# Two elementwise steps of the first units on GpSimd in place of VectorE

## The chip, the cores and the metric
The kernel runs on one core of one Trainium2 chip. The metric is the device time of one execution in microseconds, from a set of repeated runs; lower is better. A profiled execution, from which all rows below come, has its own time beside the span from its first to its last instruction. The engines are named as the profile names them: PE (TensorE), DVE (VectorE), ACT (ScalarE), POOL (GpSimd), SP (the queue that issues the DMAs).

## The reference
Three stages follow each other. A linear attention with a complex decay for each step and channel, over 4 batches, 8 heads, 768 steps and a head size of 48; a dense layer of 384 to 2048 to 384 with a piecewise quadratic activation; and a mixture of 8 experts of 384 to 1024 to 384, mixed by a table that is normalized by rows and columns in turn.

```python
# attention, for each b, h; a = a_re + i a_im
mag = sqrt(a_re**2 + a_im**2)
a_n = a * min(mag, 0.999) / (mag + 1e-6)
for t in range(768):
    S = a_n[t][:, None] * S + outer(k[t], v[t])
    y[t] = q[t] @ S.real
# dense layer on x = y with heads side by side: 3072 x 384
h = x @ w_in
g = where(h >= 1, h, where(h <= -1, 0, (h + 1)**2 / 4))
x2 = g @ w_out
# experts
P = exp(x2 @ w_gate - max); 8 times: rows to sum 1, columns to sum 1, times 3072 / 8
out = sum over e of P[:, e] * (relu(x2 @ w1[e]) @ w2[e])
```

## The kernel before
The time axis is cut into 6 chunks of 128 steps, and a chunk into two units of two batches, so there are 12 units (u = 0 to 11), each of 256 rows of the 384-wide activations. Attention and dense layer go unit by unit; the experts follow when all are done.

A unit's attention has three parts. `attn_norm` (lines 191 to 226) makes the decay's factor, `min(mag, 0.999) / (mag + 1e-6)`, once for each of the unit's two batches, and multiplies the decay tile `A` (real and imaginary part) by it at line 223. `attn_front` (233 to 335) transposes `A` to have time along the free axis (`flip`, 258), forms the products of all decays up to each step by a tree of complex multiplications (`cmul`, 277 to 287, all on VectorE from SBUF to SBUF), transposes back, and scales q and k by them (321 and 331). Its k tile `kh` has 32 columns of padding that GpSimd sets to zero (242); that tile has one buffer, so the padding of a unit is set after the state matmuls of the unit before (393) have read it. `attn_back` (339 to 430) does the attention matmuls of the chunk, masks the scores on VectorE (367, which reads PSUM), and makes the unit's input to the dense layer as two tiles, `x0h` and its rest `x0l`.

The matrix products of both later stages are made with values that are split into a rounded part and the rest of it: `gh` and `gl`, `x0h` and `x0l`, and two planes of each weight tile. Three products of such parts stand for one of full precision.

The dense layer `moe1` (473 to 529) goes over the 16 column blocks of `w_in` in 8 pairs. Each pair has 18 matmuls of line 116 into one PSUM tile; ScalarE makes the activation in three steps (488 to 490), VectorE finishes it (491, which reads PSUM and SBUF) into `t`, ScalarE rounds it into `gh` (494), and VectorE makes the rest `gl` (495). TensorE reads a pair's `gh` and `gl` two pairs later (line 498, `LAG1 = 2`; the matmuls of line 509). `t` has two buffers, `gh` and `gl` three each. During unit 0 the 16 weight tiles are loaded as well (`load_w_moe`, 449 to 471), two for a pair: a tile's raw data come by DMA into one of three staging buffers, which the decay tiles `A` use too; VectorE takes them apart in three instructions (456, 457, 460), ScalarE makes the rounded plane (464), TensorE and ScalarE the second (468 to 470).

The order of the work comes from generators. `weave` (535) draws attention steps of the coming units between the dense layer's steps of the present one, by weights that each generator yields, with `RATIO = 1.2` attention steps' weight for each of the dense layer. `step(u)` (559) runs `attn_back(u)`, `attn_front(u + 1)` and `attn_norm(u + 2)` side by side. From that order the framework's planner makes one queue for each engine, with its own durations and the order of the program as priority. Each engine then runs its queue strictly in order, an instruction waiting on semaphores for what it reads and for buffers to come free.

Before the change GpSimd sets constants, the padding of `kh`, and, from the last unit on, makes sums and differences of the experts' weights and inputs (592 to 595, 652 to 655).

Of the kernel before, what the change touches and what calls it, by code (L numbers as in the profile page):

```python
# [13 lines left out]
ALU = mybir.AluOpType  # L14
# [6 lines left out]
def scan_moe_moe(  # L21
# [14 lines left out]
    nc = tc.nc  # L36
# [20 lines left out]
    M2MIN = 0.97  # L57
    RATIO = 1.2
    NSPLIT = 1
    LAG1 = 2  # L60
    NFIRST = 2
    NWA = 10
# [40 lines left out]
    def f32(ap):  # L103
        return ap.bitcast(F32)
# [4 lines left out]
    def w2p(w, s, c0, n):  # L109
        return w[:, s, DM + c0:DM + c0 + n]  # L110

    def layer1(ps, w, xh, xl):
        n = 0
        for kc in range(KC):
            for s, x in ((0, xh), (0, xl), (1, xh)):
                nc.tensor.matmul(ps, w1p(w, s, kc), x[:, kc, :], start=(n == 0), stop=(n == 3 * KC - 1))  # L116
                n += 1

    def sinkhorn(pool, psp):
# [47 lines left out]
        out=mask, in_=mask, pattern=[[1, 128]], compare_op=ALU.is_ge,  # L167
# [23 lines left out]
    def attn_norm(u):  # L191
        if u < NSPLIT:
            yield from both(norm_part(u, 0, "ns", "nr"), norm_part(u, 1, "qh", "kh"))
        else:
            for b in range(BH):
                yield from norm_part(u, b, "ns", "nr")

    def norm_part(u, b, tag1, tag2):
        A = loaded[u, "a"]
        s12 = ap1.tile([128, 2, DM], F32, name=f"ns{u}_{b}", tag=tag1)  # L200
        r = ap1.tile([128, DM], F32, name=f"nr{u}_{b}", tag=tag2)
        s1, s2 = s12[:, 0], s12[:, 1]
        Ab = A[:, :, b * DM:(b + 1) * DM]
        nc.scalar.activation(s1, Ab[:, 0], AF.Square)
        nc.scalar.activation(s2, Ab[:, 1], AF.Square)
        nc.vector.tensor_tensor_reduce(
            out=s1, in0=s1, in1=s2, op0=ALU.add, op1=ALU.min, scale=1.0, scalar=3.0e38,
            accum_out=mins[:, u * BH + b:u * BH + b + 1],
        )
        yield 0.5  # L210
        nc.scalar.activation(s2, s1, AF.Relu, bias=c_mq)
        nc.scalar.activation(s2, s2, AF.Ln, bias=c_q)
        nc.scalar.activation(r, s2, AF.Exp, scale=-0.5, bias=c_lnh)
        nc.scalar.activation(s2, r, AF.Square, scale=2.0 / MAXMAG)
        nc.vector.tensor_tensor(out=s2, in0=s1, in1=s2, op=ALU.mult)
        yield 0.5
        nc.vector.scalar_tensor_tensor(
            out=r, in0=s2, scalar=3.0, in1=r, op0=ALU.subtract, op1=ALU.mult, reverse0=True
        )
        nc.scalar.activation(s2, r, AF.Identity, scale=-EPS / MAXMAG, bias=c_one)  # L220
        nc.vector.scalar_tensor_tensor(out=r, in0=r, scalar=1.0, in1=s2, op0=ALU.min, op1=ALU.mult)
        yield 1
        nc.vector.tensor_tensor(
            out=Ab, in0=Ab, in1=r.unsqueeze(1).to_broadcast([128, 2, DM]), op=ALU.mult
        )
        yield 1

    def parts(u):
        return [(b, 1) for b in range(BH)] if u < NSPLIT else [(0, BH)]

# [218 lines left out]
    def load_w_moe(f):  # L449
        pool = wpa if f < NWA else wpb  # L450
        if f not in raws:
            raw_w(f)
        st = raws.pop(f)
        w = pool.tile([128, 2, 2 * DM], F32R, name=f"w_m{f}", tag="w")
        lo, hi = st[:, :, 0], st[:, :, 1]
        nc.vector.tensor_scalar(out=lo, in0=lo, scalar1=29, scalar2=None, op0=ALU.logical_shift_right)
        nc.vector.scalar_tensor_tensor(
            out=lo, in0=hi, scalar=3, in1=lo, op0=ALU.logical_shift_left, op1=ALU.bitwise_or
        )
        nc.vector.scalar_tensor_tensor(  # L460
            out=lo, in0=hi, scalar=-(1 << 31), in1=lo, op0=ALU.bitwise_and, op1=ALU.bitwise_xor
        )
        xf = f32(lo)
        nc.scalar.activation(w[:, 0, :], xf, AF.Copy, scale=-(2.0 ** -126))
        for i in range(2):
            sl = slice(i * DM, (i + 1) * DM)
            ps = ps_h.tile([128, DM], F32, name=f"lo{f}_{i}", tag="h")
            nc.tensor.matmul(ps, up, xf[:, sl], start=True, stop=False)
            nc.tensor.matmul(ps, dn, w[:, 0, sl], start=False, stop=True)
            nc.scalar.activation(w[:, 1, sl], ps, AF.Copy, scale=2.0 ** -63)  # L470
        wm[f] = w

    def moe1(u):
        c, bp = divmod(u, B // BH)
        xh, xl = x0.pop(u)
        hh = {}
        NP = NF1 // 2
        for p in range(NP + LAG1):
            if p < NP:
                ps = ps_h.tile([128, 2, UT], F32, name=f"h{u}_{p}", tag="h")  # L480
                for i in range(2):
                    for f in range(min(2 * p + i + 3, NF1)):
                        if f not in wm:
                            load_w_moe(f)
                    layer1(ps[:, i, :], wm[2 * p + i], xh, xl)
                    yield 1
                t = hp.tile([128, 2, UT], F32, name=f"t{u}_{p}", tag="t", bufs=2)
                nc.scalar.activation(t, ps, AF.Relu, bias=c_one, scale=-0.25)
                nc.scalar.activation(t, t, AF.Relu, bias=c_two, scale=-1.0)
                nc.scalar.activation(t, t, AF.Square, scale=0.5)  # L490
                nc.vector.scalar_tensor_tensor(out=t, in0=ps, scalar=0.25, in1=t, op0=ALU.mult, op1=ALU.max)
                gh = hp.tile([128, 2, UT], F32R, name=f"gh{u}_{p}", tag="hh")
                gl = hp.tile([128, 2, UT], F32R, name=f"gl{u}_{p}", tag="hl")
                nc.scalar.activation(gh, t, AF.Copy)  # L494
                nc.vector.tensor_tensor(out=gl, in0=t, in1=f32(gh), op=ALU.subtract)
                hh[p] = (gh, gl)
                yield 0
            if p >= LAG1:
                gh, gl = hh.pop(p - LAG1)
                for i in range(2):  # L500
                    j = 2 * (p - LAG1) + i
                    w = wm[j]
                    for m in range(KC):
                        if j == 0 and m == 0:
                            a01 = ps_a.tile([128, 2, UT], F32, name=f"x2pa{u}", tag="m")
                            a2 = ps_a.tile([128, UT], F32, name=f"x2pb{u}", tag="m")
                            acc = (a01[:, 0], a01[:, 1], a2)
                        for n, (s, g) in enumerate(((0, gh), (0, gl), (1, gh))):
                            nc.tensor.matmul(  # L509
                                acc[m], w2p(w, s, m * 128, 128), g[:, i, :],  # L510
                                start=(j == 0 and n == 0 and m != 1), stop=(j == NF1 - 1 and n == 2 and m != 0),
                                skip_group_check=(m < 2),
                            )
                    yield 1
        lg = psp.tile([128, BH, NE], F32, name=f"lg{u}", tag="m")
        for m in range(KC):
            with tc.high_priority(60):
                xb = x0p.tile([128, UT], F32, name=f"x2b{u}_{m}", tag="x2b", bufs=2)
                nc.scalar.activation(xb, acc[m], AF.Copy, scale=0.25)
                nc.sync.dma_start(x2s[c][:, m, bp * UT:(bp + 1) * UT], xb)  # L520
            for b in range(BH):
                for o in (0, 64):
                    nc.tensor.matmul(
                        lg[o:o + 64, b, :], xb[:, b * T + o:b * T + o + 64], wg[:, m, :],
                        start=(m == 0 and b == 0), stop=(m == KC - 1 and b == BH - 1), skip_group_check=True,
                    )
        j = c * B + bp * BH
        nc.vector.tensor_copy(P[:, j:j + BH, :], lg)
        yield 1
# [20 lines left out]
    def both(*gs):  # L550
        gs = list(gs)
        while gs:
            for g in list(gs):
                try:
                    yield next(g)
                except StopIteration:
                    gs.remove(g)
# [64 lines left out]
    for u in range(NU):  # L622
        while u not in done:
            next(side)
        if u == NU - 1:
            attn.close()
            xrp = main.enter_context(tc.tile_pool(name="xrp", bufs=1, side="right", reuse_waits="tile"))
            load_x2(0)
            load_x2(1)
        weave(moe1(u), side, RATIO)  # L630
# [414 lines left out]
```

## Time and profile before

| | us |
|---|---|
| median of 3 runs | 2310.19 |
| lowest, highest | 2309.71, 2314.92 |
| profiled execution, its own time | 2307.67 |
| its span | 2305.9 |
| PE busy in the span | 2239.6 (97%) |
| PEld (weight loads) | 2145.3 (93%) |
| DVE busy | 1644.2 (71%) |
| ACT busy | 914.0 (40%) |
| POOL busy | 117.3 (5%) |

The shares are means over very different stretches. Up to about 62 us the first unit's attention runs alone; then the dense layer of unit 0 with its weight loads and the attention of unit 1; then eleven units of dense layer with attention beside it; and from about 700 us on the experts. So the rows below are taken by stretch. The profile's granted clock of PE has a mean of 0.993 over the span, and is 0.9 or more of full speed in all of the page's 40 slices but the first.

### The profile page before, as it was taken

What the parts mean: (1) busy time and instruction counts of PE and PEld (TensorE: products, weight loads), DVE (VectorE), ACT (ScalarE), POOL (GpSimd) and SP (SyncE); (2) the same over time, 40 slices, a digit from 0 to 9 for tenths busy, and PEclk for the clock granted to TensorE, in tenths of its full rate; (3) what the DMA queues carried; (4) which work ended last, traced back from release to release, by engine and by line L of the source; (5) the groups of instructions that cost most, each with busy time, mean ns of one, the idle gap of its engine ahead of it and who ended that gap; (6) DMA issues with size and microseconds to landing.
All of it is one profiled execution on the core that took longest, in us unless ns stands there. A gap on an engine that the chain in (4) does not pass through costs nothing.

```text
span 2305.9 us, 40891 instructions
## 1 busy us (share of the span) xinstructions
PE 2239.6 (97%) x16829; PEld 2145.3 (93%) x16829; DVE 1644.2 (71%) x3064; ACT 914.0 (40%) x1641; POOL 117.3 (5%) x178
## 2 busy tenths in 40 slices
PE   3789999999999999999999999999999999999998
PEld 2679999999998999999999999999999999999998
DVE  8898888887754887767866877675575576556554
ACT  5787877776566223222322322232232232222221
POOL 0000000000012010100100200010020010000000
PEclk8999999999999999999999999999999999999999
DMA  7443222211123143431423332231132222221220
GB/s 137 144 97 60 49 45 43 43 29 29 29 83 117 57 150 116 146 110 70 165 96 110 124 110 96 83 137 50 74 138 83 82 71 110 83 83 62 90 110 30
DMA packets 179795, 204.06 MB, mean 88 GB/s; under 512 B 128144, under 2 KB 168592, under 8 KB 173456
## 3 DMA queue, kind: packets, MB, share of 16 engines
q1 hardware_dynamic: 179600, 201.36, 27.2%
q8 instruction: 135, 2.21, 0.4%
q14 instruction: 60, 0.49, 0.1%
HBM read 177.75 MB, written 23.59 MB: 87 GB/s over the span
## 4 chain that ended last, share of the span: by engine, by line
PE 87%; DVE 7%; ACT 3%; DMA 1%; issue 1%; SPq 0%; POOL 0%; DVEq 0%; POOLq 0%; ACTq 0%
PE o L739 35%; PE pF L677 12%; PE pE L677 9%; PE h L116 7%; PE pG L677 6%; PE pH L677 6%; PE x2pa L509 4%; PE x2pb L509 2%; DVE M L277 1%; PE sc L365 1%; DVE M L282 1%; DVE Pk L286 1%; PE y L380 1%; PE kTps L355 1%; PE qTps L355 1%
## 5 line engine op out<-in xcount | busy, mean ns | idle before, releaser
L739 PE MATMUL o<-wB,eg 128*128 128x384 f32 x3072 | 784.2, 336 | 0.0
L739 PEld LDWEIGHTS o<-wB,eg 128*128 128x128 f32 x3072 | 547.1, 188 | 0.0
L739 PE MATMUL o<-wB,el 128*128 128x384 f32 x1536 | 515.6, 336 | 0.0
L723 ACT ACTIVATE eg<-et 128x512 fp32r<-128x512 f32 x384 | 243.0, 633 | 682.8 <-DVE et L719 412.0
L724 DVE SCALAR_TENSOR_TENSOR el<-et,eg 128x512 fp32r<-128x512 f32 x384 | 274.1, 714 | 189.0 <-ACT eg L723 186.7
L739 PEld LDWEIGHTS o<-wB,el 128*128 128x128 f32 x1536 | 288.2, 188 | 0.0
L677 PE MATMUL pE<-xop,wA 128*128 128x512 f32 (+1 forms) x1152 | 234.1, 338 | 0.0
L677 PE MATMUL pF<-xop,wA 128*128 128x512 f32 (+1 forms) x1152 | 234.1, 338 | 0.0
L116 PE MATMUL h<-x0h,w_m 128*128 128x256 f32 x1152 | 230.4, 288 | 0.9 <-ACT x0h L427 0.7
L712 DVE TENSOR_TENSOR u<-pH,sv 128x256 f32<-128x256 f32 x192 | 81.2, 423 | 208.5 <-ACT sv L711 208.3
L711 ACT ACTIVATE sv<-pH 128x256 f32<-128x256 f32 x192 | 73.9, 385 | 381.9 <-PE pH L677 381.9
L677 PEld LDWEIGHTS pE<-xop,wA 128*128 128x128 f32 x1152 | 190.0, 189 | 26.3
L677 PEld LDWEIGHTS pF<-xop,wA 128*128 128x128 f32 x1152 | 190.0, 189 | 26.3
L116 PEld LDWEIGHTS h<-x0h,w_m 128*128 128x128 f32 x1152 | 185.8, 191 | 3.7 <-ACT x0h L427 1.3
L509 PE MATMUL x2pa<-gh,w_m 128*128 128x256 f32 x768 | 179.0, 294 | 10.0 <-ACT gh L494 10.0
L677 PE MATMUL pG<-xop,wS 128*128 128x256 f32 x1152 | 169.1, 283 | 0.0
L719 DVE TENSOR_TENSOR et<-pE,sv 128x512 f32<-128x512 f32 x192 | 132.4, 690 | 48.0 <-PE pE L677 47.2
L116 PE MATMUL h<-x0l,w_m 128*128 128x256 f32 x576 | 165.4, 287 | 1.0 <-DVE x0l L428 1.0
L677 PEld LDWEIGHTS pG<-xop,wS 128*128 128x128 f32 x1152 | 152.1, 192 | 0.0
L509 PEld LDWEIGHTS x2pa<-gh,w_m 128*128 128x128 f32 x768 | 133.6, 192 | 13.4 <-ACT gh L494 11.5
L713 DVE TENSOR_TENSOR sv<-pG,u 128x512 f32<-128x512 f32 x192 | 132.6, 691 | 17.6 <-DVE u L712 0.9
L719 DVE TENSOR_TENSOR et<-pF,sv 128x512 f32<-128x512 f32 x192 | 132.2, 688 | 0.3 <-PE pF L677 0.3
(164 smaller groups left out, 3502.6 us busy)
## 6 DMA issues: line engine op xcount, KB each, us to landing
xop<-x2o SPq DMA_DIRECT2D x42, 2304.0 KB, 8.9
st_e<-in_moe_w_dram SPq DMA_DIRECT2D x64, 384.0 KB, 3.9
x2o<-xop SPq DMA_DIRECT2D x6, 2304.0 KB, 9.6
st_m<-in_moe_w_in_dram SPq DMA_DIRECT2D x16, 384.0 KB, 3.4
st_m<-in_moe_w_out_dram SPq DMA_DIRECT2D x16, 384.0 KB, 4.0
raw<-in_moe_w_in_dram SPq DMA_DIRECT2D x16, 384.0 KB, 3.5
raw<-in_moe_w_out_dram SPq DMA_DIRECT2D x16, 384.0 KB, 4.2
q<-in_q_dram SPq DMA_DIRECT2D x12, 384.0 KB, 4.1
```

Source lines behind the costliest of these rows:

```text
L116: nc.tensor.matmul(ps, w1p(w, s, kc), x[:, kc, :], start=(n == 0), stop=(n == 3 * KC - 1))
L277: nc.vector.tensor_tensor(out=m[:, x], in0=dst[:, x:x + 1].to_broadcast(shp), in1=src, op=ALU.mult)
L355: nc.tensor.transpose(ps[:D2, i, :], src[:, 4 * g + i, :], ident)
L509: nc.tensor.matmul(acc[m], w2p(w, s, m * 128, 128), g[:, i, :], start=(j == 0 and n == 0 and m != 1), stop=(j == NF1 - 1 and n == 2 and m ...
L677: nc.tensor.matmul(ps, w[:, a], op[:, b, o:o + n], start=(first and k == 0), stop=(last and k == 2), skip_group_check=True)
L711: nc.scalar.activation(sv[:, 0], H[:, 0], AF.Copy)
L712: nc.vector.tensor_tensor(out=u, in0=H[:, 1], in1=sv[:, 0], op=ALU.add)
L713: nc.vector.tensor_tensor(out=sv[:, 1:3], in0=G, in1=u.unsqueeze(1).to_broadcast([128, 2, HT]), op=ALU.add)
L719: nc.vector.tensor_tensor(out=t, in0=F, in1=sv[:, 2 * r:2 * r + 2], op=ALU.add)
L723: nc.scalar.activation(xh, tf, AF.Relu)
L724: nc.vector.scalar_tensor_tensor(out=xl, in0=tf, scalar=0.0, in1=f32(xh), op0=ALU.max, op1=ALU.subtract)
L739: nc.tensor.matmul(po[i, b], g[:, b * T:(b + 1) * T], wB[:, s, o2:o2 + DM], start=(f == 0 and n == 0), stop=(f == NF2 - 1 and n == 2),)
```

## The change
In the first four units the rest `gl` is made by GpSimd; in units 1 to 3 (`NSPLIT` is 1) the product of `A` with its factor is made by GpSimd too. Operands, tiles, buffers and the text of the generators stay as they are. That moves 4 x 8 = 32 instructions of 128x512 and 3 x 2 = 6 of 128x768.

```diff
+    NPOOL = 4
...
         nc.vector.scalar_tensor_tensor(out=r, in0=r, scalar=1.0, in1=s2, op0=ALU.min, op1=ALU.mult)
         yield 1
-        nc.vector.tensor_tensor(
+        eng = nc.gpsimd if NSPLIT <= u < NPOOL else nc.vector
+        eng.tensor_tensor(
             out=Ab, in0=Ab, in1=r.unsqueeze(1).to_broadcast([128, 2, DM]), op=ALU.mult
         )
...
                 nc.scalar.activation(gh, t, AF.Copy)
-                nc.vector.tensor_tensor(out=gl, in0=t, in1=f32(gh), op=ALU.subtract)
+                eng = nc.gpsimd if u < NPOOL else nc.vector
+                eng.tensor_tensor(out=gl, in0=t, in1=f32(gh), op=ALU.subtract)
                 hh[p] = (gh, gl)
```

## Rows read from the trace of the kernel before

**Rows 1.** Busy time by stretch: start:end, length, then each engine's busy us (instructions), PE clock, DMA.
```profile
0.00:62.00 62.00, 27.12 (x241) 20.86 (x242) 48.49 (x156) 35.95 (x74) 1.71 (x16) 0.83 0.66 128
70.00:128.00 58.00, 48.40 (x287) 39.75 (x288) 56.22 (x104) 40.42 (x72) 0.00 (x0) 0.97 0.48 154
128.00:170.00 42.00, 35.87 (x382) 31.97 (x381) 37.47 (x86) 33.84 (x68) 0.13 (x1) 1.00 0.49 84
170.00:330.00 160.00, 157.63 (x1737) 150.47 (x1736) 139.65 (x289) 125.62 (x238) 0.38 (x3) 1.00 0.23 45
330.00:2305.90 1975.90, 1965.02 (x14154) 1897.70 (x14152) 1358.95 (x2426) 670.61 (x1179) 115.06 (x158) 1.00 0.26 89
```

**Rows 2.** VectorE in order of time, 100 to 116 us: start, duration, what, shapes.
```profile
100.18 0.95 DVE L223 TENSOR_TENSOR A<-A,nr 128x768 f32<-128x768 f32 x1
101.05 0.95 DVE L457 SCALAR_TENSOR_TENSOR st_m<-st_m 128x768 int32<-128x768 int32 x1
...
112.09 0.97 DVE L460 SCALAR_TENSOR_TENSOR st_m<-st_m 128x768 int32<-128x768 int32 x1
...
115.21 0.70 DVE L495 TENSOR_TENSOR gl<-t,gh 128x512 fp32r<-128x512 f32 x1
115.81 0.97 DVE L460 SCALAR_TENSOR_TENSOR st_m<-st_m 128x768 int32<-128x768 int32 x1
```

**Rows 3.** TensorE in order of time at 113 us, in brackets its idle time before.
```profile
113.16 1.25 PE L468 MATMUL lo<-st_m,up 128*128 128x384 f32 x3 [2.12 <-issue]
```

**Rows 4.** VectorE's groups, 70 to 128 us: busy us, mean ns, idle before.
```profile
L456 DVE TENSOR_SCALAR st_m<-st_m 128x768 int32<-128x768 int32 x11 | 6.2, 565 | 1.5 <-DMA st_m<-in_moe_w_out_dram 1.5
...
L495 DVE TENSOR_TENSOR gl<-t,gh 128x512 fp32r<-128x512 f32 x6 | 4.1, 691 | 0.0
L491 DVE SCALAR_TENSOR_TENSOR t<-h,t 128x512 f32<-128x512 f32 x6 | 4.1, 691 | 0.0
L223 DVE TENSOR_TENSOR A<-A,nr 128x768 f32<-128x768 f32 x2 | 1.9, 966 | 0.0
```

**Rows 5.** VectorE's groups that read PSUM, 128 to 170 us.
```profile
L491 DVE SCALAR_TENSOR_TENSOR t<-h,t 128x512 f32<-128x512 f32 x4 | 2.8, 697 | 2.3 <-ACT t L490 2.3
L367 DVE TENSOR_TENSOR at<-sc,mask 128x512 f32<-128x512 f32 x4 | 2.8, 695 | 0.0
```

**Rows 6.** Two of VectorE's groups, 170 to 330 us.
```profile
L495 DVE TENSOR_TENSOR gl<-t,gh 128x512 fp32r<-128x512 f32 x23 | 15.9, 689 | 1.8 <-ACT gh L494 1.8
L491 DVE SCALAR_TENSOR_TENSOR t<-h,t 128x512 f32<-128x512 f32 x22 | 15.2, 689 | 1.1 <-ACT t L490 1.1
```

**Rows 7.** GpSimd in order of time, at 677 us and 722 to 726 us.
```profile
676.92 0.74 POOL L594 TENSOR_TENSOR xt<-x2r 128x256 f32<-128x256 f32 x1
...
722.13 0.74 POOL L594 TENSOR_TENSOR xt<-x2r 128x256 f32<-128x256 f32 x1
722.83 1.18 POOL L593 TENSOR_TENSOR xt<-x2r,xt 128x256 f32<-128x256 f32 x1
724.09 1.32 POOL L595 TENSOR_TENSOR xt<-x2r,xt 128x256 f32<-128x256 f32 x1
```

**Rows 8.** VectorE in order of time, in the same two places.
```profile
677.38 0.69 DVE L491 SCALAR_TENSOR_TENSOR t<-h,t 128x512 f32<-128x512 f32 x1 [2.85 <-ACT t L490]
...
722.17 1.25 DVE L666 TENSOR_TENSOR wS<-sf,wS 128x512 fp32r<-128x512 f32 x1 [1.39 <-ACT wS L665]
723.48 1.34 DVE L666 TENSOR_TENSOR wA<-st_e,wA 128x768 fp32r<-128x768 f32 x1
724.75 1.21 DVE L495 TENSOR_TENSOR gl<-t,gh 128x512 fp32r<-128x512 f32 x1
725.88 0.95 DVE L666 TENSOR_TENSOR wB<-st_e,wB 128x768 fp32r<-128x768 f32 x1
```

**Rows 9.** Writers and readers of `gl`, 0 to 200 us: min/median/max ns, first to last start.
```profile
L509 PE MATMUL x2pa<-gl,w_m x48: 277/283/386, 79.2 to 195.0; 128*128 128x256 f32 x48
...
L495 DVE TENSOR_TENSOR gl<-t,gh x14: 683/690/711, 71.8 to 197.4; 128x512 fp32r<-128x512 f32 x14
```

**Rows 10.** GpSimd's waits, 0 to 330 us: total us, times, longest.
```profile
POOL kh L242 <- PE z L393: 243.9, 4, 95.8
```

## The prediction
> **What bounds the kernel now.** I read the busy time by stretch first [rows 1]. From 330 us to the end TensorE is busy 1965.02 of 1975.90 us, so nothing done to VectorE there can matter, and the change does not touch those units. From 170 to 330 us TensorE is busy 157.63 of 160.00 us: it is still the bound, but VectorE is busy 139.65 us beside it and has only 20.35 us left. The stretch from 70 to 128 us, which is most of the first unit's dense layer, is different: TensorE has 48.40 of 58.00 us, VectorE 56.22. From 128 to 170 us, where the second unit's attention is finished, TensorE has 35.87 of 42.00 us and VectorE 37.47. So 9.6 and 6.1 us of idle TensorE lie where the change acts, and in the first of the two VectorE is full.
>
> The timelines show how that becomes TensorE's time [rows 2, 3]. The line-460 instruction that finishes one weight tile starts at 112.09 us and lasts 0.97, to 113.06; TensorE's next matmul, which reads that tile (`lo<-st_m`), starts at 113.16 after an idle of 2.12 us. The row puts the idle down to "issue", but the end of line 460 is what it follows by 0.1 us. VectorE's queue runs in order, so everything in front of line 460 is paid by TensorE. Line 495, one of the two moved instructions, stands right in front of the next line 460 (115.21, next at 115.81), and line 223, the other, right in front of a line 457 (100.18, next at 101.05).
>
> **What is removed.** From start to next start one `gl` (line 495, 128x512) holds VectorE for 0.60 us and one norm product (line 223, 128x768) for 0.87 us [rows 2]. 32 `gl` and 6 products move. By stretch: 6 `gl` and 2 products lie in 70 to 128 us [rows 4]; 23 `gl` lie in 170 to 330 us [rows 6], and that leaves 3 `gl` and the two products of unit 3 in 128 to 170 us. The two products of unit 1 lie before 62 us or right at it, where VectorE has 48.49 of 62.00 us [rows 1]; I count these at nothing, with at most 2 x 0.87 us either way.
> - 70 to 128 us: 6 x 0.60 + 2 x 0.87 = 5.34 us off VectorE.
> - 128 to 170 us: 3 x 0.60 + 2 x 0.87 = 3.54 us.
> - 170 to 330 us: 23 x 0.60 = 13.8 us.
>
> **What is added.** The trace of before shows no GpSimd instruction of these shapes, but it shows GpSimd adding and subtracting 128x256 tiles, some while VectorE works [rows 7, 8]. Three of them start at 722.13, 722.83 and 724.09 us. VectorE's three instructions beside them (128x512, 128x768, 128x512, both inputs in SBUF) start at 722.17, 723.48 and 724.75, and the next starts at 725.88: 3.71 us for what costs 0.60 + 0.87 + 0.60 = 2.07 us alone. So 1.64 us were lost to three GpSimd instructions, 0.55 us each, and GpSimd's own last from 0.74 to 1.18 and 1.32 us in the same place. The two take turns. An instruction of VectorE that reads PSUM is not held: line 491 at 677.38 lasts 0.69 us beside a GpSimd instruction that runs from 676.92 to 677.66 [rows 7, 8], the mean of all line 491 from 70 to 128 us being 691 ns [rows 4].
>
> Scaled by the elements, a `gl` on GpSimd takes 2 x 0.55 = 1.10 us from VectorE and a product 3 x 0.55 = 1.65 us. These are estimates. Bounds: from below nothing, if the larger form finds gaps that the small one did not; from above GpSimd's own step, 0.70 us from 722.13 to 722.83 for 256 elements, so 1.40 and 2.10 us. I take 1.10 and 1.65, since those are measured on the victim. They cost nothing while VectorE is idle or reads PSUM:
> - 70 to 128 us: idle 1.78 us, line 491 6 x 0.60 = 3.6 us, together 5.4 of 58, or 9%. Added (6 x 1.10 + 2 x 1.65) x 0.91 = 9.0 us; removed 5.34; net **+3.6 us**. VectorE is the bound here, so I put all of it on the path.
> - 128 to 170 us: idle 4.53 us, lines 491 and 367 8 x 0.60 = 4.8 us [rows 5], together 22%. Added (3 x 1.10 + 2 x 1.65) x 0.78 = 5.1 us; removed 3.54; net +1.6 us. TensorE is idle for 6.1 of 42 us and busy else, VectorE is the last in only part of these waits: I take half, **+0.8 us**.
> - 170 to 330 us: idle 20.35 us, line 491 22 x 0.60 = 13.2 us, together 21%. Added 25.3 x 0.79 = 20.0 us; removed 13.8; net +6.2 us of VectorE. Its cover is the 20.35 us in which VectorE is idle beside a full TensorE: **0**; if that cover is in the wrong places, up to 6.2 us.
>
> One rule of the Trainium skill bears on the cover. Line 456, with one SBUF input, takes 565 ns for 768 elements [rows 4], against 0.97 us for the two-input line 457 or 460 of the same size [rows 2]. The page "VectorE: DVE Perf Modes" (What auto-detection actually checks) says that a one-source instruction between SBUF operands may use both ports, and "SBUF — State Buffer" (Who interferes with whom) that it then shuts GpSimd out and is shut out by it; no row shows a line 456 beside GpSimd. By that rule it gives no cover, which is how the sum treats it. If it did, its 6.2 us in 70 to 128 us would raise the cover to 20% and the net there would be +2.6 in place of +3.6 us.
>
> **What the added waits hold up.** A `gl` is first read by TensorE at 79.2 us [rows 9], 7.4 us after the first was made at 71.8, because line 498 reads it two pairs later; 0.5 to 1 us more for its making is covered. GpSimd's queue also holds the memset of line 242, which waits for the state matmuls of the unit before, 243.9 us in four waits [rows 10]. A `gl` queued behind it would wait too, but the same two-pair lag covers up to 7 us. I count it at nothing. No DMA moves with the change, and SP's queue issues the same transfers.
>
> **Sum.** 3.6 + 0.8 = +4.4 us on the profiled execution's own 2307.67 us (span 2305.9 and 1.8 around it): 2312.1. The median of the runs shown, 2310.19, lies 2.5 us above that execution, so the forecast as a median is 2314.6 us. The change's size is near what can be told here: 0.3%, about 7 us, is what a measurement of this kernel tells from no change.
>
> **Rivals.**
> - *Relief.* GpSimd's instructions slip into gaps and VectorE only loses work: 5.34 us off the full stretch and half of 3.54 off the next, 7.1 us, so 2303.1 us. For it: VectorE is full there and TensorE waits for it [rows 1 to 3]. Against it: the turns taken at 722 to 726 us [rows 7, 8].
> - *Spill.* The place is 170 to 330 us, the price 6.2 us more on VectorE, and it decides if the front parts of units 3 to 5 come late and TensorE, in order, stands before their transposes. Then 4.4 + 0.8 (all of the middle stretch) + 6.2 = +11.4, so 2321.6 us, slower. For it: VectorE is busy 87% there and has only 20 us. Against it: TensorE is busy 98.5% of it today [rows 1], with work of the dense layer ready between.
> - *Nothing seen.* The planner puts the instructions in another order, the weight loads (line 460) come earlier because VectorE's queue holds less, and loss and relief cancel: 2310 us, within 2 us. For it: VectorE still has to wait for landings in this stretch, 1.5 us before line 456 [rows 4]. Against it: nothing in the rows frees VectorE on balance.
>
> **How the numbers follow.** Forecast 0.45 (its own range 2311 to 2318), spill 0.22, nothing seen 0.18, relief 0.15. Slower than 2317.1 us: nearly all of the spill and a small part of the forecast's upper end, 0.28. Faster than 2303.3 us: about half of the relief, and some for orders that I don't foresee, 0.12. Within 0.3%: 0.60. The range of 2303 to 2321 reaches to the relief below and to most of the spill above.
>
> **What would show it.** In the changed profile lines 457 and 460 from 70 to 128 us should last longer than 0.97 us wherever a GpSimd `gl` runs, about half a microsecond each time; GpSimd's `gl` should last from 1.2 to above 1.8 us; TensorE's idle from 70 to 170 us should grow from 15.7 to about 20 us, and from 170 us on stay as it is. If lines 457 and 460 keep 0.96 us, the price is wrong and the relief is right. If TensorE's idle from 170 to 330 us grows past 2.4 us by more than 3, it is the spill. If the first reads of `gl` wait on GpSimd, the two-pair lag did not cover, and I was wrong about its queue.

## The result, and the profile after

The changed kernel takes 2338.3 us (median of 5 runs, 2335.5 to 2338.9) against 2311.7 us for the kernel before in the same runs (2309.7 to 2314.9). The ratio is 1.0115, with a 95% interval of 1.0103 to 1.0126: slower by 26.6 us, where 4.4 us were forecast, and outside the range given. The profiled execution has a span of 2336.9 us against 2305.9. In the lines of the changed kernel 116 is 117, 223 is 225, 242 is 244, 456 to 460 are 458 to 462, 491 is 493, 495 is 498 and 509 is 512.

First the busy time by stretch, as in [rows 1] (start:end, length, then busy us and instructions of PE, PEld, DVE, ACT, POOL, then the granted clock of PE, DMA share and GB/s):
```profile
0.00:62.00 62.00, 27.53 (x186) 21.39 (x186) 45.99 (x151) 34.05 (x69) 3.98 (x16) 0.78 0.65 128
70.00:128.00 58.00, 42.99 (x231) 34.54 (x229) 51.71 (x88) 35.23 (x64) 12.09 (x7) 0.88 0.42 138
128.00:170.00 42.00, 34.78 (x343) 30.19 (x342) 32.14 (x62) 28.63 (x57) 6.20 (x4) 0.98 0.59 118
170.00:330.00 160.00, 144.33 (x1470) 136.14 (x1468) 133.05 (x248) 116.92 (x221) 39.50 (x24) 0.97 0.23 43
330.00:2336.90 2006.90, 1992.62 (x14523) 1924.16 (x14521) 1383.05 (x2474) 689.88 (x1218) 118.72 (x163) 1.00 0.25 88
```
From 170 to 330 us TensorE was idle for 2.4 us and is now idle for 15.7; from 70 to 170 us 15.7 has become 22.2. VectorE's idle time grew too: 1.8 to 6.3 us in 70 to 128, 20.4 to 27.0 in 170 to 330. Over the whole span VectorE is busy 1649.3 us (1644.2 before) though it has 38 instructions fewer. It was relieved of work, kept its busy time, and both engines wait more. Where an instruction lasts longer beside GpSimd than the median of its form in the kernel before, the text calls it held, and the extra time a hold.

GpSimd's groups over the whole span (busy us, mean ns of one, idle time before and what ended it):
```profile
L498 POOL TENSOR_TENSOR gl<-t,gh 128x512 fp32r<-128x512 f32 x32 | 54.7, 1710 | 194.5 <-ACT gh L496 187.3 <-DMA st_m<-in_moe_w_in_dram 7.2
L225 POOL TENSOR_TENSOR A<-A,nr 128x768 f32<-128x768 f32 x6 | 12.3, 2049 | 61.4 <-DVE nr L222 61.4
```
A `gl` lasts 1.27 us at best and 3.97 at worst, where VectorE takes 0.69 [rows 4]. What TensorE waits for between 170 and 360 us (us in total, times, longest), the five largest:
```profile
PE x2pa L512 <- POOL gl L498: 4.3, 4, 1.3
PE tP L260 <- DVE x0l L430: 4.1, 2, 2.7
PE x2pa L512 <- POOL kh L244: 1.8, 1, 1.8
PE h L117 <- DVE x0l L430: 1.6, 1, 1.6
PE y L386 <- DVE at L369: 1.5, 1, 1.5
```
In the kernel before there was one row here, `tP` for `x0l`, 2.3 us. Of the new waits 6.1 us are for a GpSimd `gl` (the row that names `kh` is one as well, shown below), and most of the rest are for VectorE instructions whose own work is unchanged.

Three places show the three mechanisms. The first is a `gl` that comes late, at 227 us. GpSimd, TensorE and VectorE in order of time (start, duration, what; in brackets the idle time before):
```profile
227.18 3.97 POOL L498 TENSOR_TENSOR gl<-t,gh 128x512 fp32r<-128x512 f32 x1 [7.18 <-ACT gh L496]
231.10 0.12 POOL L244 MEMSET kh<- 128x32 f32 x1
```
```profile
231.21 0.39 PE L512 MATMUL x2pa<-gl,w_m 128*128 128x256 f32 x1 [1.76 <-POOL kh L244]
```
```profile
227.20 0.57 DVE L222 SCALAR_TENSOR_TENSOR nr<-nr,ns 128x384 f32<-128x384 f32 x1
227.67 0.56 DVE L288 TENSOR_TENSOR Pk<-M 128x378 f32<-128x378 f32 x1
228.13 0.56 DVE L289 TENSOR_TENSOR Pk<-M 128x378 f32<-128x378 f32 x1
228.59 0.97 DVE L225 TENSOR_TENSOR A<-A,nr 128x768 f32<-128x768 f32 x1
229.46 0.56 DVE L207 CUSTOM_DVE_ANT_0 ns<-ns 128x384 f32<-128x384 f32 x1
229.94 0.10 DVE L207 DVE_READ_ACCUMULATOR2_ANT mins<- 128x1 f32 x1
229.94 0.57 DVE L400 TENSOR_TENSOR Tst<-z,Tst 96x384 f32<-96x384 f32 x1
```
VectorE runs from SBUF to SBUF without a gap and at its usual durations. GpSimd's `gl` ends at 231.15, 1.2 us, about one `gl` at its best, after line 400 started at 229.94, the first VectorE instruction since 227.18 with an input in PSUM. The reader of this `gl` stands right behind, and the memset's 0.12 us has no part in the wait, since line 512 reads no `kh`: it is only GpSimd's last event before TensorE goes on. At 281.44 us VectorE holds GpSimd in the same way: a `gl` lasts 3.12 us and ends 1.22 us after a line 369, which reads PSUM, started at 283.34. It is no rule, though: at 265.04 another `gl` lasts 2.50 us beside instructions from SBUF to SBUF alone, and the one of these that starts at 266.32 lasts 1.32 us in place of 0.24.

The second is a VectorE instruction held by GpSimd, at 86 us, and what stands behind it (GpSimd, VectorE, TensorE):
```profile
85.55 1.80 POOL L225 TENSOR_TENSOR A<-A,nr 128x768 f32<-128x768 f32 x1 [9.50 <-DVE nr L222]
```
```profile
85.88 1.90 DVE L458 TENSOR_SCALAR st_m<-st_m 128x768 int32<-128x768 int32 x1 [0.41 <-DMA st_m<-in_moe_w_out_dram]
87.70 0.32 DVE L288 TENSOR_TENSOR Pk<-M 128x96 f32<-128x96 f32 x1
87.87 0.95 DVE L459 SCALAR_TENSOR_TENSOR st_m<-st_m 128x768 int32<-128x768 int32 x1
88.73 0.32 DVE L289 TENSOR_TENSOR Pk<-M 128x96 f32<-128x96 f32 x1
88.90 0.95 DVE L462 SCALAR_TENSOR_TENSOR st_m<-st_m 128x768 int32<-128x768 int32 x1
```
```profile
89.95 2.26 PE L470 MATMUL lo<-st_m,up 128*128 128x384 f32 x3 [4.45 <-issue]
```
Line 458 lasts 1.90 us in place of 0.565 [rows 4] and ends 0.43 us after GpSimd's instruction; line 462 ends 1.3 us later for it, at 89.85, and TensorE starts at 89.95. So 1.3 of its 4.45 us of idle time are the hold; the rest is the split itself, which could not start before the tile's data had landed, at 85.76. It is the same kind of wait, for another tile, as the 2.12 us in [rows 3].

The third is the order of the queues, which the planner made anew. VectorE right behind the first `x0l`, in the changed kernel and then in the kernel before:
```profile
66.77 0.08 DVE L207 DVE_READ_ACCUMULATOR2_ANT mins<- 128x1 f32 x1
72.11 0.69 DVE L493 SCALAR_TENSOR_TENSOR t<-h,t 128x512 f32<-128x512 f32 x1 [5.26 <-ACT t L492]
72.72 0.55 DVE L458 TENSOR_SCALAR st_m<-st_m 128x768 int32<-128x768 int32 x1
```
```profile
68.86 0.56 DVE L456 TENSOR_SCALAR st_m<-st_m 128x768 int32<-128x768 int32 x1 [4.58 <-DMA st_m<-in_moe_w_out_dram]
69.46 0.96 DVE L457 SCALAR_TENSOR_TENSOR st_m<-st_m 128x768 int32<-128x768 int32 x1
70.34 0.68 DVE L491 SCALAR_TENSOR_TENSOR t<-h,t 128x512 f32<-128x512 f32 x1
```
Before, the split of the next weight tile, the fifth, stood ahead of `t`; after, it stands behind a `t` that ScalarE isn't done with. That wait by itself costs little here, since the tile's data landed only at 72.43 us (68.74 before). What follows costs more: the first `lo` matmul of this tile starts 7.3 us after the landing, at 79.69, where it was 3.4 us before, at 72.11. Not counting the 38 moved instructions, 613 places of TensorE's queue, about 400 of VectorE's, 336 of ScalarE's and 11 of SP's hold another instruction than before.

### The profile page after: what moved, and what is told of

The parts are those of the page before. It is cut to its first block, busy times and chain, and to the rows that moved or that the text cites. A ratio compares the mean times of both kernels' runs of the same rounds, so it can differ in the third digit from the quotient of the medians.

```text
span 2336.9 us, 40943 instructions
## 1 busy us (share of the span) xinstructions
PE 2249.9 (96%) x16829; PEld 2153.1 (92%) x16829; DVE 1649.3 (71%) x3026; ACT 911.2 (39%) x1641; POOL 182.5 (8%) x216
## 4 chain that ended last, share of the span: by engine, by line
PE 85%; DVE 7%; ACT 3%; DMA 2%; issue 1%; POOL 1%; SPq 0%; DVEq 0%; POOLq 0%; ACTq 0%
PE o L742 34%; PE pF L680 11%; PE pE L680 9%; PE h L117 6%; PE pG L680 6%; PE pH L680 6%; PE x2pa L512 4%; PE x2pb L512 2%; DVE M L279 2%; PE sc L367 1%; DMA st_e<-in_moe_w_dram 1%; DVE Pk L288 1%; DVE M L284 1%; PE y L382 1%; PE y L386 1%
## 5 line engine op out<-in xcount | busy, mean ns | idle before, releaser
L512 PEld LDWEIGHTS x2pa<-gh,w_m 128*128 128x128 f32 x768 | 135.1, 194 | 13.3 <-ACT gh L496 11.2
L716 DVE TENSOR_TENSOR sv<-pG,u 128x512 f32<-128x512 f32 x192 | 132.6, 691 | 17.6 <-DVE u L715 0.9
```

Of the source, the lines that this page charges most:

```text
L512: nc.tensor.matmul(acc[m], w2p(w, s, m * 128, 128), g[:, i, :], start=(j == 0 and n == 0 and m != 1), stop=(j == NF1 - 1 and n == 2 and m ...
L716: nc.vector.tensor_tensor(out=sv[:, 1:3], in0=G, in1=u.unsqueeze(1).to_broadcast([128, 2, HT]), op=ALU.add)
```

## The experiments

All ratios are to the kernel before in runs on the same chip, with a 95% interval; its median was 2308.7 to 2311.8 us in the four sets of runs.

| kernel | moved work on | order of the queues | us | ratio |
|---|---|---|---|---|
| order of before, written out | VectorE | old | 2312.6 | 1.0001 [0.9992, 1.0010] |
| GpSimd in the old order | GpSimd | old | 2321.4 | 1.0052 [1.0035, 1.0068] |
| VectorE in the new order | VectorE | new | 2327.5 | 1.0075 [1.0059, 1.0092] |
| the change | GpSimd | new | 2338.3 | 1.0115 [1.0103, 1.0126] |
| idle subtracts on GpSimd | VectorE | old | 2330.2 | 1.0079 [1.0065, 1.0093] |
| only `gl` moved | GpSimd | planner's | 2338.5 | 1.0121 [1.0104, 1.0138] |
| only the product moved | GpSimd | planner's | 2317.6 | 1.0033 [1.0019, 1.0048] |

Three explanations stand against each other: the new order of the queues costs; TensorE waits for a `gl` that GpSimd hands over later; or GpSimd's use of SBUF holds VectorE, which the expectations call the port. To part the engine from the order, an order was written out: at the end of the program each instruction gets a dependency, without a semaphore, on the one that stood before it on its engine in a recorded order. `text` is the packed record, a list of steps from one instruction's number to the next; dots stand for lines of code left out.
```diff
+    for d in json.loads(zlib.decompress(base64.b85decode(text))):
+        at += d
+        i = here[at]
...
+        if i.engine in queue:
+            tc.add_manual_dep(
+                i, queue[i.engine],
+                mybir.DependencyInfo(mybir.DependencyClass.NoSync, mybir.DependencyReason.DATA), reason="pin",
+            )
+        queue[i.engine] = i.name
```

**The control: before in its own order, written out** (run after the two that follow it here).

> The kernel before, with each engine's queue fixed to the order that the planner gave it anyway: nothing is moved. Both theories (order and shared port) expect 2311 us, within 3. Above 2317 us the fixing itself would cost time, and what the two kernels with fixed orders showed (2321 with GpSimd in the old order, 2328 with VectorE in the new) would have to be lowered by as much.

1.0001: writing the order out costs nothing that can be measured. Its profiled execution, 2.4 us above its median, serves below as a second look at the kernel before, and it corrects a reading. Same order, same median, yet a span of 2313.3 us against 2305.9, and these rows:
```profile
70.00:128.00 58.00, 46.98 (x255) 37.72 (x253) 52.62 (x100) 38.83 (x70) 0.00 (x0) 0.88 0.48 155
128.00:170.00 42.00, 36.33 (x356) 31.95 (x357) 35.95 (x80) 30.59 (x61) 0.12 (x1) 0.93 0.56 95
170.00:330.00 160.00, 158.42 (x1733) 151.89 (x1733) 141.07 (x295) 126.62 (x239) 0.38 (x3) 1.00 0.23 43
```
The granted clock is 0.88 and 0.93 here where it was 0.97 and 1.00 in [rows 1]. The 7.4 us lie in TensorE's busy time (2249.0 us of the span against 2239.6), not in its idle time (64.3 against 66.3): the same instructions took longer, where the clock was lower. So a clock of 0.88 comes without the change too. Against this look the span of the changed kernel is 23.6 us longer, and TensorE's idle time 22.7 us longer (87.0 against 64.3): the loss is waiting. The busy times of the whole span, in the control and in the changed kernel:
```profile
PE 2249.0 (97%) x16829; PEld 2153.3 (93%) x16829; DVE 1646.0 (71%) x3064; ACT 912.6 (39%) x1641; POOL 115.6 (5%) x178
PE 2249.9 (96%) x16829; PEld 2153.1 (92%) x16829; DVE 1649.3 (71%) x3026; ACT 911.2 (39%) x1641; POOL 182.5 (8%) x216
```

**The change in the old order.**

> The changed kernel with every engine's queue held to the order of the kernel before; only the engine of the 38 moved instructions differs from before. Three theories. Order: the planner's new order costs the 26.6 us, the engine nothing, so this is within 5 us of before (about 2312). Hand-over: GpSimd makes gl later (1.4 to 4.1 us behind gh in the changed trace, 0.7 to 1.8 before) and TensorE stands before its readers, whatever the order: at least 2325. Port: VectorE is held for what GpSimd takes, 24.5 us in the changed trace, against 24.4 us of work removed, so about 0 and 2312 too. I expect a part: +8 to +14, 2320 to 2326, since five of the first eleven gl of before were read within 0.2 us of their end.

Within what was expected: +0.52%. Waits of TensorE for a GpSimd `gl` shrink from 8.7 us in seven places to 1.4 us in two. VectorE's holds stay, 25.8 us from 62 to 360 us. One of them is at 336 us, where a `gl` (from 336.14 us, 1.26 us long) holds line 241 (222 of the changed kernel, 0.55 us alone) in front of `x0l`; it makes 0.66 of the 3.12 us that TensorE waits:
```profile
336.60 1.22 DVE L241 SCALAR_TENSOR_TENSOR nr<-nr,ns 128x384 f32<-128x384 f32 x1 [0.73 <-ACT ns L240]
337.74 1.01 DVE L449 TENSOR_TENSOR x0l<-x0ps,x0h 128x512 fp32r<-128x512 f32 x2
```
```profile
338.48 1.09 PE L279 MATMUL tP<-ident,Pk 128*128 128x128 f32 x8 [3.12 <-DVE x0l L449]
```

**All work on VectorE, in the new order.**

> The kernel before, all 38 instructions on VectorE, with every engine's queue held to the order that the planner made for the changed kernel. Order theory: near the changed kernel, 2330 or more. Hand-over or port theory: near before, 2312, within 5 us. I expect between, +8 to +16, 2320 to 2328: unit 0 should lose most of what it lost with the change, since the longer waits of TensorE there (4.5 us before lo, 3.3 before x2pa) stand before VectorE's and ScalarE's results, not GpSimd's.

+0.75%, at the upper end of what was expected: more than GpSimd's instructions cost in the old order, with none of the moved work on GpSimd. The two add up to 1.27%, near the change's 1.15%. One sign of the new order is what VectorE waits for at `t` between 62 and 360 us: after, VectorE in the new order, and the control (us in total, times, longest).
```profile
DVE t L493 <- ACT t L492: 13.8, 7, 5.3
```
```profile
DVE t L510 <- ACT t L509: 14.4, 8, 5.4
```
```profile
DVE t L510 <- ACT t L509: 4.1, 3, 2.2
```
In the new order `t` stands early in VectorE's queue, with other work behind it, and TensorE waits for that work: 2.68 us for `x0l` at 227 us, where VectorE had stood idle 0.75 us for a `t` and 0.98 us for a `gl` ahead of `x0l`. The busy times from 170 to 360 us show the same split between engine and order (columns as in [rows 1]; before, GpSimd in the old order, VectorE in the new order, the change):
```profile
170.00:360.00 190.00, 187.63 (x2054) 179.65 (x2053) 165.56 (x352) 148.84 (x280) 0.38 (x3) 1.00 0.25 47
170.00:360.00 190.00, 183.28 (x1926) 174.78 (x1926) 159.54 (x295) 144.11 (x271) 37.00 (x27) 0.99 0.25 47
170.00:360.00 190.00, 178.09 (x1868) 168.63 (x1867) 157.41 (x315) 141.79 (x265) 0.37 (x3) 0.98 0.22 43
170.00:360.00 190.00, 172.38 (x1811) 162.91 (x1808) 155.60 (x295) 136.24 (x258) 44.73 (x29) 0.98 0.20 39
```
TensorE is idle for 2.4, 6.7, 11.9 and 17.6 us: 4.3 us more by GpSimd alone, 9.5 us by the order alone, 15.2 us by both.

**The port by itself: subtractions that nobody reads.**

> The kernel before in its old order, VectorE keeps all its work, and GpSimd subtracts gh from itself in two halves of 128x256 behind each of the 32 gl of units 0 to 3, into a spare tile that nothing reads. So GpSimd uses SBUF about as much as in the change, hands nothing over, and VectorE is relieved of nothing. Shared port: VectorE is held by up to 64 x 0.55 = 35 us with no relief against it, 9 to 13 us of it in 62 to 170 us where it is full, so the time is 2319 to 2331 us and lines 457 and 460 beside GpSimd last 1.5 us and more. Hand-over (the loss with GpSimd in the old order came from gl being ready later): nobody waits for the spare tile, so at most +3 us, 2311 to 2314 us.

```diff
+    def beside(a):
+        for j in range(2):
+            x = ap1.tile([128, UT], F32, name=f"spare{len(apart)}", tag="spare")
+            apart.add(nc.gpsimd.tensor_tensor(out=x, in0=a[:, j, :], in1=a[:, j, :], op=ALU.subtract).ins.name)
...
                 nc.vector.tensor_tensor(out=gl, in0=t, in1=f32(gh), op=ALU.subtract)
+                if u < 4:
+                    beside(f32(gh))
```
`apart` keeps these subtractions out of the recorded order. The result is 2330.2 us, +0.79%: what the expectation calls the shared port, and not the hand-over. From 60 to 360 us no wait of TensorE, VectorE or ScalarE is put down to GpSimd, so what costs is that VectorE's instructions last longer. Lines 457 and 460 beside GpSimd lasted up to 1.39 us, less than the 1.5 that was expected. VectorE's `gl` beside them lasts 865 ns on average where the control has 687 (groups of 62 to 360 us, the idle subtracts first):
```profile
L525 DVE TENSOR_TENSOR gl<-t,gh 128x512 fp32r<-128x512 f32 x32 | 27.7, 865 | 2.0 <-ACT gh L524 1.8
```
```profile
L514 DVE TENSOR_TENSOR gl<-t,gh 128x512 fp32r<-128x512 f32 x36 | 24.7, 687 | 2.2 <-ACT gh L513 2.2
```
Summed over all of VectorE's instructions, each against the median of its form before, it is held 5.0 us in 62 to 170 us and 12.7 in 170 to 360. Units 1 to 3 take 13.4 us longer than in the control, about as much as VectorE is held there.

The length of each unit, from its first dense matmul to the next unit's, worked out from the start times of these matmuls:

| us | unit 0 starts | unit 0 | 1 | 2 | 3 | 4 |
|---|---|---|---|---|---|---|
| before | 62.6 | 96.2 | 57.1 | 55.6 | 55.6 | 54.1 |
| before, order written out | 65.1 | 100.3 | 58.0 | 55.7 | 55.6 | 54.0 |
| the change | 65.1 | 107.6 | 66.3 | 62.3 | 58.2 | 54.2 |
| GpSimd, old order | 63.7 | 103.0 | 59.3 | 56.9 | 60.2 | 54.0 |
| VectorE, new order | 63.6 | 102.8 | 65.4 | 61.4 | 56.1 | 54.1 |
| idle subtracts | 65.3 | 103.9 | 62.1 | 60.7 | 59.9 | 54.1 |

The loss ends with unit 3 in every kernel. (Up to unit 0 the kernels also differ by the clock, as the two rows of before show.) Of the change's, two thirds lie in units 1 to 3 (17.5 us over the control), which were forecast at nothing.

**Each half alone**, the planner free.

> Only gl of units 0 to 3 on GpSimd, the norm product on VectorE, order left to the planner. Units 1 to 3 lost 19.6 of the 32.5 us in the changed trace and hold no moved product after 174 us, so by the hand-over theory 2328 to 2336; if the products of units 1 to 3 cause it, near 2312.

> Only the norm product of units 1 to 3 on GpSimd, gl on VectorE, order left to the planner. Six instructions, held or holding at 1.65 us each against 0.87: at most +5 us by the port theory (2312 to 2317); by the order theory anything up to +13, what unit 0 lost.

Moving `gl` alone already costs 1.21%, as much as the whole change and above what was expected; 399 places of TensorE's queue change with it. The six products alone cost 0.33% (2317.6 us, just above the 2317 that the port theory allowed). The wait at `t` is no measure of the loss: with `gl` alone moved it is 4.6 us, near the control's 4.1, and with the products alone 7.6 us. The halves don't add up (1.54 against 1.15), since each brings an order of its own.

**Which queue's order costs**, all with the work on GpSimd. Only the named queues are held to the old order; the planner lays the others anew around them:

> The changed kernel with TensorE's queue alone fixed to the order of before; VectorE and ScalarE keep what the planner makes around it (some 340 and 270 places differ from before). If what costs in the new order is TensorE doing a pair's 12 matmuls on gh and gl ahead of the lo matmuls, and with that late staging buffers, most of the order's 17 us goes: 2320 to 2327 us. If it is the order of VectorE and ScalarE, it stays at 2333 to 2340 us.

> The changed kernel with the queues of VectorE and ScalarE fixed to the order of before, and TensorE's free (some 290 places differ from before). The other way round: 2333 to 2340 us if TensorE's order costs, 2320 to 2327 us if that of VectorE and ScalarE does. If neither this kernel nor the one with TensorE's queue fixed comes down by more than 4 us, it is the match between the queues and no single one of them.

> The changed kernel with VectorE's queue alone fixed to the order of before. With the queues of VectorE and ScalarE fixed it took 2329 us, with none 2338, with all 2321. If VectorE's order is what costs in units 1 to 3 (x0l queued behind instructions that wait for ScalarE, as at 226 us of the kernel with VectorE in the new order), it comes to 2326 to 2332 us; if it is ScalarE's, it stays at 2335 to 2341.

> The changed kernel with ScalarE's queue alone fixed to the order of before. The other way round: 2335 to 2341 us if VectorE's order costs, 2326 to 2332 us if ScalarE's does. If this and the kernel with VectorE's queue fixed both stay above 2335 us, the two queues have to match each other and neither order is bad by itself.

Old order for | us | ratio
---|---|---
TensorE | 2340.9 | 1.0128 [1.0112, 1.0143]
VectorE | 2339.0 | 1.0121 [1.0105, 1.0136]
ScalarE | 2344.0 | 1.0144 [1.0128, 1.0160]
VectorE and ScalarE | 2329.1 | 1.0079 [1.0065, 1.0092]
all | 2321.4 | 1.0052 [1.0035, 1.0068]

My first guess, TensorE doing a pair's 12 matmuls ahead of the `lo` matmuls, falls: giving TensorE its old order gains nothing. So does "VectorE's order alone" (2326 to 2332 expected, 2339.0 measured), and the old order of ScalarE alone makes it slower still. Of the sets tried only the two queues that hand `t`, `gh` and `gl` to each other gain, and only together: somewhat more than half of what all queues gain, and not quite down to the 2327 us that was expected. So the two have to match; what in the match costs stays open.

**Is any other order worse, or only one made without this work on VectorE?** The weight between attention and dense layer was changed, in both kernels, and at that weight the two mixed cases were run again.
```diff
-    RATIO = 1.2
+    RATIO = 1.4
```

> The kernel before with the same RATIO of 1.4. If the order of before is one good order among worse ones, this is slower than before, 2316 to 2330 us; if the time hangs little on the order as long as VectorE does the work, it is 2311 us, within 4.

> The changed kernel with RATIO 1.4 in place of 1.2, so that the attention of the next unit stands earlier in the program's order, and with it x0l. If the order's loss is a matter of where attention stands against the dense layer, a new weight gets back a good part of it: 2318 to 2330 us. If it is the price of GpSimd's longer instructions, whatever the weight, it stays at 2334 us or more.

> RATIO 1.4, the moved work on GpSimd, every queue in the order that the planner makes at 1.4 with the work on VectorE. If an order fits that was planned with the full load on VectorE (which GpSimd's hold on SBUF gives it in any case), this is about 0.5% slower than before, 2319 to 2326 us, some 10 us under the changed kernel at 1.4 (2335.6). If the old order of 1.2 was just a lucky one, and the price is in GpSimd's instructions, it is 2332 to 2338 us.

> RATIO 1.4, all work on VectorE, every queue in the order that the planner makes at 1.4 with the work on GpSimd. If an order planned for a lighter VectorE is what costs, 2322 to 2332 us, as at 1.2 (2327.5). If the order by itself is harmless and only GpSimd's instructions cost, 2311 us within 4.

| RATIO 1.4 | us | ratio |
|---|---|---|
| work on VectorE, its order | 2311.3 | 0.9999 [0.9990, 1.0008] |
| work on GpSimd, the order planned with it on VectorE | 2322.0 | 1.0055 [1.0040, 1.0070] |
| work on VectorE, the order planned with it on GpSimd | 2325.0 | 1.0069 [1.0054, 1.0084] |
| work on GpSimd, its order | 2335.6 | 1.0102 [1.0087, 1.0118] |

The same table at another order, within 0.15%. The new weight gains the changed kernel almost nothing (2335.6 us). The old order was not a lucky one: another that was planned with the work on VectorE is as fast. Both that were planned with it on GpSimd are slower, whichever engine then does it, and VectorE waits 10.0 to 14.4 us for ScalarE's `t` in these four kernels, 4.1 us or less in the control and in before at RATIO 1.4.

Shown is the split: 0.3 to 0.55% by GpSimd's instructions, and 0.5 to 0.75% by the order, by which step is taken first. Why the planner's order is worse is argued, not shown: it may plan as if VectorE had become lighter by the moved work. It has not. VectorE was relieved of 32 x 0.60 + 6 x 0.87 = 24.4 us, and from 62 to 360 us its other instructions lasted 24.5 us longer than the medians of their forms before, nearly all of it in 28 of them. The durations that the planner uses were not seen, and a rival was not tested: that it takes GpSimd's `gl` for longer and lays other work ahead of its readers. No kernel here beats the one before.

## Why the prediction was wrong

Two steps that decided the time failed: the planner's new order, which the sum put at nothing and which costs 0.75% by itself (the last point below), and the cover from 170 to 330 us, put at 0, where units 1 to 3 lost 7.1 us with the order kept. The 3.6 + 0.8 us of the first two stretches can't be told from these profiles, since the clock there differs between executions: with GpSimd in the old order unit 1 starts 1.3 us later than in the control, and 7.9 us later than in the first profile of before.

**What bounds the kernel: half right.** VectorE is full beside the first dense layer, and TensorE's `lo` waits on it. The step that failed is "Its cover is the 20.35 us in which VectorE is idle beside a full TensorE: **0**". Of VectorE's waits there in the kernel before, 13.7 us end with ScalarE and 3.6 with TensorE; since the queue goes in order, nothing from later in it moves into them. That they are no cover is shown twice: with GpSimd in the old order units 1 to 3 take 7.1 us more than in the control (176.4 against 169.3), and the idle subtracts give 12.7 us of held VectorE time and 13.4 us of longer units. The exception that I priced ("up to 6.2 us") and the spill rival had the right place and, in the old order, nearly the size. TensorE's idle time from 170 to 330 us grew by 13.3 us, and by my own sign, over 3 us, that is the spill; but most of that growth is the order's, as the four rows from 170 to 360 us show. The spill's mechanism, TensorE in front of the transposes, is 4.9 of the 17.6 us idle there.

**What is removed: right**, 24.4 us with unit 1's products. But as much came back by holds. The Trainium skill, "Perfetto Trace Analysis" (Optimizing Scalar/DVE Operations), warns that moving work between these two engines might not help, since they share a port; the trace agrees, with 24.4 us relieved and 24.5 held.

**What is added: too high, and it was not what decided.** The sum had 34.1 us of holds after cover, the trace has 24.5. GpSimd's `gl` lasted 1.27 to 3.97 us, where 1.2 to above 1.8 was said. Lines 459 and 462 lasted 1.06 us on average instead of 0.96, by one instruction each that was held for some 1.07 us (2.02 us at 74.85, 2.03 at 92.23), and not by half a microsecond wherever a `gl` runs:
```profile
L459 DVE SCALAR_TENSOR_TENSOR st_m<-st_m 128x768 int32<-128x768 int32 x10 | 10.6, 1059 | 0.1
L462 DVE SCALAR_TENSOR_TENSOR st_m<-st_m 128x768 int32<-128x768 int32 x9 | 9.6, 1068 | 0.0
```
"The two take turns", read from three instructions at 722 to 726 us [rows 7, 8], is no rule: at 227 us VectorE went on and GpSimd did not get in. VectorE's net load is then about nothing, and by the load alone the time would not have changed. The kernel is still 0.5% slower in the old order. The likely reason is that a hold is paid where it falls (line 241 ahead of `x0l`) and a relief is only gained where VectorE ends last; this was seen in places and not summed over all of them.

**The one-input rule: right.** The sum gave line 456 (now 458) no cover, and the row at 85.88 us shows it held for GpSimd's whole instruction. The Trainium skill, "SBUF — State Buffer" (Who interferes with whom), says that such an instruction in its two-port mode and GpSimd shut each other out; the trace agrees, 1.90 us against 0.565.

**The lag of two pairs: wrong.** I took the distance between the first `gl` and its reader, 7.4 us, for all [rows 9]. For others the reader stood right behind: in the trace of before the time from the end of a `gl` to its first matmul is 0.06 to 0.35 us for the last two pairs of unit 0 and the first three of unit 1 (four of these five are under 0.2 us, not five as I wrote ahead of the run in the old order). The wait for GpSimd's `gl` is 8.7 us in seven places of the changed kernel, and by my own sign that proves the step wrong. GpSimd's memset, which I weighed, held nothing: its waits fell from 243.9 us [rows 10] to 29.6.

**"No DMA moves": wrong in time.** SP issues the same transfers, but some of them later: from 64 us on the third and fourth pair of weight loads are issued at 81.28 and 84.33 us, against 75.19 and 78.59 in the kernel before. In the control they go out at 77.93 and 81.75, so only 3.4 and 2.6 us of this are the change's; the second pair, at 70.31 against 70.22, isn't late by it.

**The planner's order: seen, with the wrong sign.** "Nothing seen" had the planner's new order cancel loss and relief, at 2310 us. Order alone costs 0.75% (0.69% at the other weight), the largest term, and none of my cases had it as a loss. What in the order costs is not known. With it the forecast's missing 22 us are placed: 0.5% by GpSimd's work in the old order, where 0.2% was forecast, the other 0.6% by the order where nothing was.

## What to carry to other kernels

Moving an instruction under a planner can move every queue, as it did here; try the move in the old order as well, which parts the two causes in one run. An engine's idle time is cover only if its queue has something to put there: look at what stands behind the wait, in order. Between VectorE and GpSimd relief and hold can nearly cancel (24.4 against 24.5 us here) and the move can still cost, since the holds land on other instructions than the relief.

## What the runs showed of the hardware

- GpSimd does not always get its turn after one VectorE instruction: a `gl` that needs 1.27 us alone took 3.97, and another 3.12, and both ended 1.2 us after the start of VectorE's first instruction with an input in PSUM. In other places the hold was the other way round (1.90 us for 0.565).
- Two executions of one and the same order differed by 7.4 us in span, with a granted clock of 0.97 and 0.88 from 70 to 128 us, so a single profile's clock in the first stage says little. The lower level shows in the trace of the changed kernel: after an idle time of TensorE of 3.31 us up to 73.55 us and another of 1.76 up to 76.11, its matmuls of 128x256 start 0.21 us apart, against 0.12 at 228 us; the granted clock is 0.54 from 76.1 to 80 us, so these are the levels of 1.2 and 2.4 GHz.
- 64 subtractions of 128x256 on GpSimd, read by nobody, cost the kernel 18 us of 2310.
